# The opening of a Fourier-mixing and SoLU kernel: four z buffers, another order of loads, TensorE transposes for the first units, small operations moved to ScalarE

## The chip, the cores and the metric

The kernel runs on one core of one Trainium2 chip. The metric is the time of one execution on the device in microseconds (us), as the median of several executions.

## The reference

```python
def reference(x, moe_w_in, moe_w_out, moe_g_ln):   # x: 8 x 3136 x 256
    X = np.fft.fft(np.fft.fft(x, axis=1), axis=2).real
    x = X.reshape(8 * 3136, 256)
    h = x @ w_in                                    # 256 x 1024
    e = np.exp(h - h.max(-1, keepdims=True))
    solu = h * (e / (e.sum(-1, keepdims=True) + 1e-09))
    ln = (solu - mean(solu)) / np.sqrt(var(solu) + 1e-06) * g_ln
    return ln @ w_out                               # 1024 x 256
```

The real part of a two-dimensional Fourier transform of each of 8 batches, then a layer of 256 to 1024 to 256 features with a softmax-weighted activation and a normalization.

## The kernel before

The batches are handled in four pairs. The 3136 rows are 49 times 64. For one pair, the rows come in eight chunks. Each chunk is *folded* (mirrored rows and features are added and subtracted, which halves the transform), multiplied by a 49-point table (`transform1`), copied by ScalarE out of PSUM (the memory into which TensorE writes its results) into a buffer `z`, and written to DRAM (`zd`). When all eight chunks are in DRAM, `turn` reads them back in another order (`g`). From there on the work goes by *units*, 25 per pair, 100 in all: second transform (`q`), up-projection (`ps_h`), `ev` (the first VectorE operation of a unit) and `join` on VectorE, `exp` on ScalarE, product on VectorE, square on ScalarE, transpose, and four units later the down-projection. While one pair's units run, the next pair's chunks are folded and transformed in between. Only the first pair has nothing to lie beside, and the weights have to be loaded, narrowed from 64-bit words to float32 and multiplied in that same time: this is the *opening*.

```python
def fold_features(o, i):
    up, down = i[:, :, 1:128], i[:, :, 255:128:-1]
    nc.vector.tensor_tensor(out=o[:, :, 1:128], in0=up, in1=down, op=ALU.add)
    nc.vector.tensor_tensor(out=o[:, :, 129:256], in0=up, in1=down, op=ALU.subtract)
    nc.vector.tensor_copy(out=o[:, :, 0:129:128], in_=i[:, :, 0:129:128])   # the "corner copy"

def transform1(pr, s):
    c, l = divmod(2 * s, CH)                     # chunk, row in it
    if l == 0:
        pr.z = zpool.tile([ZR, CH, D], FP32, tag="z", name="z")      # a pool of 2
    # ... matmuls of F with y = pr.y[c] into ps
    nc.scalar.copy(pr.z[:, l : l + 2, :], ps[0:ZR])
    if l == CH - 2:
        nc.sync.dma_start(out=pr.zd[:, c * CH : (c + 1) * CH, :], in_=pr.z)

# the opening
for c in range(NC):                              # 8 chunks of the first pair
    add_mirror(first, c, nc.vector)
    fold(first, c)
    # ... load of chunk c + 6
    for s in range(CH // 2):
        transform1(first, c * CH // 2 + s)
    if c < 4:
        weights.narrow_in(c)
    # ...
    elif 3 < c < 7:
        weights.product_in(c - 4)
    if c == 5:
        weights.load_out()
weights.place_table()
turn(first, 0)
for i in range(2):
    weights.narrow_out(i)

# the units (cut): i = 0 .. 103
even(cur, up(cur, 0)); odd = up(cur, 1)          # ev on VectorE
take2(nxt, transform2(...)); spread(nxt)
join(cur, odd); expo(cur)
ahead_pe(ahd, cur.k1)                            # transform1 of the next pair
ps_o = [down(old, s) for s in old.signs]         # old = unit i - 4
product(cur, s); square(cur, s); turn_blocks(cur, s)
# ... transposes finished by DMA, statistics
ahead(ahd, cur.k1)                               # loads and folds of the next pair
```

Of the kernel before, what the change touches and what calls it, by code (L numbers as in the profile page):

```python
# [7 lines left out]

# [25 lines left out]
def kernel(  # L34
# [46 lines left out]
    ones = const.tile([P, P], FP32, name="ones")  # L81
    neg_half = const.tile([P, 2], FP32, name="neg_half")
# [33 lines left out]
    def fold_features(o, i):  # L116
        up, down = i[:, :, 1:128], i[:, :, 255:128:-1]
        nc.vector.tensor_tensor(out=o[:, :, 1:128], in0=up, in1=down, op=ALU.add)
        nc.vector.tensor_tensor(out=o[:, :, 129:256], in0=up, in1=down, op=ALU.subtract)  # L119
        nc.vector.tensor_copy(out=o[:, :, 0:129:128], in_=i[:, :, 0:129:128])  # L120
# [19 lines left out]
    def transform1(pr, s):  # L140
# [6 lines left out]
        if l == 0:  # L147
            pr.z = zpool.tile([ZR, CH, D], FP32, tag="z", name="z")
# [69 lines left out]
    def join(t, ps):  # L218
# [9 lines left out]
        nc.vector.tensor_scalar(out=t.neg[:, 0:n], in0=t.nmax[:, 0:n], scalar1=-1.0, scalar2=None, op0=ALU.mult)  # L228
# [39 lines left out]
    class Batch:  # L268


        def __init__(self):
            self.v = fpool.tile([P, 2, FF, 2], FP32, tag="v", name="v32", bufs=2)
            self.uT = fpool.tile([P, 2, KF, 4, 64], FP32, tag="uT", name="uT", bufs=2)
# [6 lines left out]
    def move_blocks(batch, units):  # L280
# [3 lines left out]
        for i in range(4):  # L284
            for q in range(4):
                a, b = slice(32 * i, 32 * i + 32), slice(32 * q, 32 * q + 32)
                nc.sync.dma_start(out=uT[b, i], in_=v[a, q])
# [69 lines left out]
    class Weights:  # L357
# [24 lines left out]
        def load_table(self):  # L382
            self.T = fpool.tile([P, NK, N2], FP32, tag="v", name="T_raw", bufs=2)
            for b in range(2):
                nc.sync.dma_start(out=self.T[b * N2 : (b + 1) * N2], in_=t_tab)

        def place_table(self):
            for b in range(2):
                r = slice(b * N2, (b + 1) * N2)
                nc.scalar.copy(T[r, :, r], self.T[r])  # L390
# [17 lines left out]
        def load_out(self):  # L408
            raw = fpool.tile([P, 2, KF, 4, 64], FP32, tag="uT", name="raw_out", bufs=2)
            self.raw = raw.rearrange("p w c i m -> p (w c i m)").bitcast(I32)  # L410
            for c in range(KF):
                load_piece(moe_w_out, self.raw[:, 2 * c * D : 2 * (c + 1) * D], Wo[:, c], c, 0, D)
# [7 lines left out]
        def centre(self):  # L420
# [5 lines left out]
            for c in range(KF):  # L426
                nc.gpsimd.tensor_tensor(out=Wo[:, c, :], in0=Wo[:, c, :], in1=wbar, op=ALU.subtract)  # L427
# [24 lines left out]
    with tc.manual_schedule():  # L452
        pairs = [Pair(p) for p in range(NP)]
        first, weights = pairs[0], Weights()
        nc.sync.dma_start(out=idx, in_=mirror)

        rooms = {}
        for c in range(2, 6, 2):
            room = fpool.tile([P, 2, KF, 4, 64], FP32, tag="uT", name="room", bufs=2)
            room = room[0:PR].rearrange("p w c i m -> p (w c i m)").rearrange("p (a n) -> p a n", a=4)  # L460
            rooms[c], rooms[c + 1] = [room[:, i] for i in (0, 1)], [room[:, i] for i in (2, 3)]
        load(first, 0)
        nc.sync.dma_start(out=F, in_=f_tab)
        weights.load_in()
        weights.piece_in(0)
        for c in range(1, 4):
            load(first, c, rooms.get(c))
            weights.piece_in(c)
        weights.load_tables()
        for c in range(4, 6):  # L470
            load(first, c, rooms[c])
        nc.vector.memset(ones, 1.0)
# [3 lines left out]
        for c in range(NC):  # L476
            add_mirror(first, c, nc.vector)
            fold(first, c)
            if c + 6 < NC:
                load(first, c + 6)  # L480
            for s in range(CH // 2):
                transform1(first, c * CH // 2 + s)
            if c < 4:
                weights.narrow_in(c)
            if c == 2:
                weights.load_table()
            elif c == 3:
                weights.mid()
            elif 3 < c < 7:
                weights.product_in(c - 4)  # L490
            if c == 5:
                weights.load_out()
        weights.place_table()
        turn(first, 0)
        for i in range(2):
# [6 lines left out]
        lag = 4  # L502
        for i in range(len(units) + lag):
# [4 lines left out]
            last = i >= len(units) - 2  # L508
            if i > lag:
                store(units[i - lag - 1])  # L510
            if cur:
                if i % 2 == 0:
                    batch = Batch()
# [3 lines left out]
            if nxt:  # L517
                take2(nxt, transform2(pairs[nxt.p], nxt.k1))
                spread(nxt)
            if cur:  # L520
# [6 lines left out]
            if cur:  # L527
                for s in cur.signs:
                    product(cur, s)
                for s in cur.signs:  # L530
                    square(cur, s)
                    turn_blocks(cur, s)
            if old:
                scale(old, 0, ps_o[0])
            if cur:
                if last:
                    move_blocks(batch, slice(cur.w, cur.w + 1))
                elif cur.w:
                    move_blocks(batch, slice(0, 2))
                stats(cur)  # L540
            if i < 2:
                weights.narrow_out(i + 2)
            elif i == 2:
# [84 lines left out]
```

## Time and profile before

| | before |
|---|---|
| median | 1234.15 us (3 runs, 1233.82 to 1235.59) |
| span of the profiled run | 1231.2 us |
| last z issued to DRAM | 66.25 us |
| g (first read back) issued | 71.27 us |
| ev of unit 0, VectorE | 81.93 us |
| first transform of the second pair (the "border") | 133.03 us |
| first up-projection of the steady stretch | 139.01 us |
| TensorE's wait in the tail | 2.49 us |

The prediction below shows the views it rests on. One more belongs to the argument: TensorE's timeline in the opening before the change (start, duration, engine, line, operation, tiles, shapes, count, and in brackets the idle time before it and what released it).

```profile
44.58 3.70 PE L158 MATMUL ps<-y,F 98*100 98x258 f32 x8 [3.58 <-DVE y L120]
...
52.93 1.89 PE L158 MATMUL ps<-y,F 98*100 98x258 f32 x8
...
58.10 1.89 PE L158 MATMUL ps<-y,F 98*100 98x258 f32 x8
```

The eight matmuls of one chunk take 3.70 us when TensorE runs at half speed and 1.89 us at full speed; the trace's record of the granted clock has 0.5 from 30.45 us to 50.93 and 1.0 from there to 68.00. So the two late chunks ran at full speed: the weight products stood between them, and TensorE did not pause from 44.58 us on. GpSimd then issues the read back of the transformed rows:

```profile
71.27 2.41 POOL L170 DMA_DIRECT2D g<-zd  x4 [47.83 <-DMA zd<-z]
```

### The profile page before, as it was taken

What the parts mean: (1) busy time and instruction counts of PE and PEld (TensorE: products, weight loads), DVE (VectorE), ACT (ScalarE), POOL (GpSimd) and SP (SyncE); (2) the same over time, 40 slices, a digit from 0 to 9 for tenths busy, and PEclk for the clock granted to TensorE, in tenths of its full rate; (3) what the DMA queues carried; (4) which work ended last, traced back from release to release, by engine and by line L of the source; (5) the groups of instructions that cost most, each with busy time, mean ns of one, the idle gap of its engine ahead of it and who ended that gap; (6) DMA issues with size and microseconds to landing.
All of it is one profiled execution on the core that took longest, in us unless ns stands there. A gap on an engine that the chain in (4) does not pass through costs nothing.

```text
span 1231.2 us, 15674 instructions
## 1 busy us (share of the span) xinstructions
PE 1159.5 (94%) x4664; PEld 875.5 (71%) x4664; DVE 929.2 (75%) x1383; ACT 612.6 (50%) x1151; POOL 542.2 (44%) x964
## 2 busy tenths in 40 slices
PE   2755899999999999999999999999999999999997
PEld 1423577777777777777777777777777777777786
DVE  6658887777777887787677887777777788778770
ACT  1223555555554555555454565565554555555551
POOL 2014755444453554544364554544453333333331
PEclk9677899999999999999999999999999999999999
DMA  9737899797899798886899899987899677776765
GB/s 230 205 118 132 156 177 162 163 169 138 147 185 181 144 172 175 165 171 115 151 189 193 141 174 173 162 168 134 150 176 163 113 125 128 122 135 106 133 111 106
DMA packets 476372, 189.57 MB, mean 154 GB/s; under 512 B 444566, under 2 KB 458142, under 8 KB 476288
## 3 DMA queue, kind: packets, MB, share of 16 engines
q1 hardware_dynamic: 462464, 150.02, 70.1%
q0 software_dynamic: 13824, 38.55, 12.0%
q8 instruction: 38, 0.62, 0.2%
q14 instruction: 46, 0.38, 0.1%
HBM read 44.78 MB, written 38.80 MB: 68 GB/s over the span
## 4 chain that ended last, share of the span: by engine, by line
PE 88%; DVE 6%; DMA 2%; issue 2%; POOL 1%; ACT 1%; POOLq 0%; DVEq 0%; ACTq 0%
PE ps_o L293 53%; PE ps_h L209 26%; PE ps L158 4%; PE ps L181 3%; DVE h L223 1%; PE wps L405 1%; DVE u L242 1%; DMA xb<-in_x_dram,idx 1%; ACT u L234 1%; DVE tmp L331 1%; DVE v L278 1%; POOL Wo L427 1%; DVE y L119 0%; DVE tmp L344 0%; DMA zd<-z 0%
## 5 line engine op out<-in xcount | busy, mean ns | idle before, releaser
L293 PE MATMUL ps_o<-Wo,uT 128*128 128x256 f32 x3136 | 694.0, 379 | 2.5 <-DMA uT<-v 2.5
L293 PEld LDWEIGHTS ps_o<-Wo,uT 128*128 128x128 f32 x3136 | 612.4, 197 | 64.7 <-issue 3.6
L209 PE MATMUL ps_h<-Wi,q 128*128 128x512 f32 x800 | 367.0, 602 | 12.7 <-DVE ev L215 12.7
L242 DVE SCALAR_TENSOR_TENSOR u<-h,u 128x1024 f32<-128x1024 f32 x196 | 233.6, 1228 | 139.3 <-ACT u L234 139.3
L234 ACT ACTIVATE u<-h,neg 128x1024 f32<-128x1024 f32 x196 | 223.7, 1142 | 223.6 <-DVE neg L228 223.6
L251 ACT ACTIVATE h<-u,nmean 128x1024 f32<-128x1024 f32 x196 | 223.6, 1142 | 130.2 <-POOL nmean L244 130.2
L244 POOL TENSOR_SCALAR nmean<-usum 128x1 f32<-128x1 f32 x196 | 126.9, 648 | 363.6 <-DVE u L242 363.3
L209 PEld LDWEIGHTS ps_h<-Wi,q 128*128 128x128 f32 x800 | 154.4, 194 | 165.7 <-issue 156.3
L223 DVE CUSTOM_DVE_ANT_0 h<-ev,ps_h 128x1024 f32<-128x1024 f32 x196 | 231.7, 1219 | 44.6 <-PE ps_h L209 39.2
L278 DVE STREAM_TRANSPOSE v<-u 128x1024 f32<-128x1024 f32 x200 | 238.1, 1234 | 0.1
L215 DVE SCALAR_TENSOR_TENSOR ev<-w_mid,r,ps_h 128x1024 f32<-128x1024 f32 x100 | 127.6, 1276 | 58.4 <-PE ps_h L209 55.3
L187 ACT COPY q<-ps 128x256 f32<-128x256 f32 x100 | 37.1, 371 | 180.4 <-PE ps L181 173.5
L305 POOL DMA_INDIRECT out_dram<-ot,idx x96 | 102.7, 1069 | 44.0 <-issue 24.0
L158 PE MATMUL ps<-y,F 98*100 98x258 f32 (+3 forms) x288 | 76.4, 402 | 36.5 <-DVE y L120 36.1
L263 POOL TENSOR_SCALAR v<-ssq 128x2 f32<-128x2 f32 (+1 forms) x100 | 27.8, 278 | 169.4 <-ACT h L251 169.4
L181 PEld LDWEIGHTS ps<-T,g 128*128 128x128 f32 x400 | 60.9, 194 | 58.1 <-issue 55.9
L298 ACT ACTIVATE ot<-ps_o,rs 128x256 f32<-128x256 f32 x196 | 80.9, 457 | 27.2 <-PE ps_o L293 27.2
L158 PEld LDWEIGHTS ps<-y,F 98*100 98x100 f32 x288 | 47.2, 183 | 51.4 <-DVE y L120 26.6
L266 POOL TENSOR_TENSOR rs<-v,neg_half 128x2 f32<-128x2 f32 (+1 forms) x100 | 72.9, 729 | 7.8
L170 POOL DMA_DIRECT2D g<-zd x80 | 47.8, 604 | 56.0 <-DMA zd<-z 47.8
L181 PE MATMUL ps<-T,g 128*128 128x128 f32 x400 | 61.6, 278 | 10.8 <-DMA g<-zd 10.8
L161 ACT COPY z<-ps 100x512 f32<-100x512 f32 x64 | 36.3, 570 | 42.4 <-PE ps L158 25.2
(58 smaller groups left out, 421.7 us busy)
## 6 DMA issues: line engine op xcount, KB each, us to landing
uT<-v SPq DMA_DIRECT2D x784, 128.0 KB
zd<-z SPq DMA_DIRECT2D x32, 400.0 KB
g<-zd POOLq DMA_DIRECT2D x80, 160.0 KB, 5.4
out_dram<-ot SPq DMA_DIRECT2D x100, 128.0 KB
xa<-in_x_dram SPq DMA_DIRECT2D x28, 392.0 KB
raw_in<-in_moe_w_in_dram SPq DMA_DIRECT2D x4, 512.0 KB
raw_out<-in_moe_w_out_dram SPq DMA_DIRECT2D x8, 256.0 KB
uT<-v SPq DMA_DIRECT2D x32, 64.0 KB
```

The source lines that it names most:

```text
L158: nc.tensor.matmul(o[..., cs], F[:, 2 * t + h, :], i[..., cs], start=first, stop=True, skip_group_check=True)
L181: nc.tensor.matmul(ps[:, h * P : (h + 1) * P], g[:, k, h * P : (h + 1) * P], T[:, k1, :], start=(h == 0), stop=True, skip_group_check=True)
L209: nc.tensor.matmul(ps[:, fs], t.q[:, c * P : (c + 1) * P], Wi[:, c, fs], start=True, stop=True)
L215: nc.vector.scalar_tensor_tensor(out=t.ev, in0=w_mid, scalar=t.r, in1=ps, op0=ALU.mult, op1=ALU.add)
L223: nc.vector.tensor_tensor_reduce(out=t.h[s], in0=t.ev, in1=ps, scale=1.0, scalar=-3.0e38, op0=ALU.subtract if s else ALU.add, op1=ALU.max, ...
L234: nc.scalar.activation(out=t.u[s], in_=t.h[s], func=ACT.Exp, bias=t.neg[:, s : s + 1], accum_out=t.esum[:, s : s + 1])
L242: nc.vector.scalar_tensor_tensor(out=t.u[s], in0=t.h[s], scalar=1.0, in1=t.u[s], op0=ALU.mult, op1=ALU.mult, accum_out=t.usum[:, s : s + 1])
L244: nc.gpsimd.tensor_scalar(out=t.nmean[:, s : s + 1], in0=t.usum[:, s : s + 1], scalar1=-1.0 / FF, scalar2=None, op0=ALU.mult)
L251: nc.scalar.activation(out=t.h[s], in_=t.u[s], func=ACT.Square, bias=t.nmean[:, s : s + 1], accum_out=t.ssq[:, s : s + 1])
L278: nc.vector.transpose(out=t.batch.v[:, t.w, :, o], in_=t.u[s])
L293: nc.tensor.matmul(ps, uT[:, c, :, s], Wo[:, c, :], start=(c == 0), stop=(c == KF - 1))
L305: dma = nc.gpsimd.indirect_dma_start(out=out, out_offset=bass.IndirectOffsetOnAxis(ap=idx[:, i : i + 1], axis=0), in_=t.ot[s], in_offset=None)
```

## The change

Its intent is a shorter opening: do not let ScalarE wait for one of two z buffers, load what is needed first, take half of w_out out of the way of the last z writes, let TensorE transpose the first four units (VectorE sets their pace), and relieve VectorE of small operations. The diff, cut to its core:

```diff
 def fold_features(o, i):
-    nc.vector.tensor_copy(out=o[:, :, 0:129:128], in_=i[:, :, 0:129:128])
+    nc.scalar.copy(o[:, :, 0:129:128], i[:, :, 0:129:128])
 # transform1
-    pr.z = zpool.tile([ZR, CH, D], FP32, tag="z", name="z")
+    if pr.p == 0 and c % 2:
+        z = fpool.tile([P, FF], FP32, tag="u", name="z_u", bufs=2)
+        pr.z = z[0:ZR].rearrange("p (l d) -> p l d", l=CH)
+    else:
+        pr.z = zpool.tile([ZR, CH, D], FP32, tag="z", name="z")
 # join
-    nc.vector.tensor_scalar(out=t.neg[:, 0:n], in0=t.nmax[:, 0:n], scalar1=-1.0, ...)
+    nc.scalar.mul(out=t.neg[:, 0:n], in_=t.nmax[:, 0:n], mul=-1.0)
+def turn_whole(t):              # units 0 to 3: 8 blocks of 128x128 for each sign
+    for s in t.signs:
+        for half in range(2):
+            ps = ps_m.tile([P, n, P], FP32, tag="m", name="ps_t")
+            for c in range(n):
+                nc.tensor.matmul(ps[:, c, :], t.u[s][:, ...], ident, is_transpose=True, ...)
+            nc.scalar.copy(uT[:, half * n : (half + 1) * n, :, s], ps)
 # load_table: one copy of the table instead of two
 # load_out: w_out in two transfers of four row blocks, load_out(0) and load_out(1)
 # centre
-    for c in range(KF):
-        nc.gpsimd.tensor_tensor(out=Wo[:, c, :], in0=Wo[:, c, :], in1=wbar, op=ALU.subtract)
+    nc.vector.tensor_tensor(out=Wo, in0=Wo, in1=wbar (broadcast), op=ALU.subtract)
 # the opening (the loads are also reordered: w_in pieces ahead of x chunks, tables last)
 for c in range(NC):
+    if c < 4:
+        weights.narrow_in(c)
     add_mirror(first, c, nc.vector)
     fold(first, c)
+    if c == 1:
+        weights.load_table()
+    elif c == 3:
+        weights.place_out(); weights.load_out(0); weights.mid(); weights.scale_out()
     for s in range(CH // 2):
         transform1(first, c * CH // 2 + s)
-    if c < 4: weights.narrow_in(c)
-    elif 3 < c < 7: weights.product_in(c - 4)
-    if c == 5: weights.load_out()
+weights.load_out(1)
+turn(first, 0)
 weights.place_table()
-turn(first, 0)
-for i in range(2): weights.narrow_out(i)
+for h in range(3): weights.product_in(h)
+for i in range(4): weights.narrow_out(i)
 # units 0 to 3: turn_whole for the unit before, ahead of join; no turn_blocks, no move_blocks
 # the last unit's moves alternate between SyncE and GpSimd
```

(Cuts and condensations marked by comments; helper definitions left out.)

More of the change, by code (lines that the diff above doesn't have):

```diff
@@ L7 @@
 from concourse._compat import with_exitstack
+from concourse.masks import make_identity
 FP32 = mybir.dt.float32
@@ L81 @@
     ones = const.tile([P, P], FP32, name="ones")
+    ident = const.tile([P, P], FP32, name="ident")
     neg_half = const.tile([P, 2], FP32, name="neg_half")
@@ L227, in join @@
         t.neg = small.tile([P, 2], FP32, tag="neg", name="neg")
-        nc.vector.tensor_scalar(out=t.neg[:, 0:n], in0=t.nmax[:, 0:n], scalar1=-1.0, scalar2=None, op0=ALU.mult)
+        nc.scalar.mul(out=t.neg[:, 0:n], in_=t.nmax[:, 0:n], mul=-1.0)
     def expo(t):
@@ L268, with __init__ @@
     class Batch:
-        def __init__(self):
-            self.v = fpool.tile([P, 2, FF, 2], FP32, tag="v", name="v32", bufs=2)
+        def __init__(self, by_blocks):
+            if by_blocks:
+                self.v = fpool.tile([P, 2, FF, 2], FP32, tag="v", name="v32", bufs=2)
             self.uT = fpool.tile([P, 2, KF, 4, 64], FP32, tag="uT", name="uT", bufs=2)
@@ L278, in turn_blocks, with move_blocks @@
             nc.vector.transpose(out=t.batch.v[:, t.w, :, o], in_=t.u[s])
-    def move_blocks(batch, units):
+    def turn_whole(t):
+        uT = t.batch.uT[:, t.w].rearrange("p c i (n s) -> p c (i n) s", s=2)
+        n = KF // 2
+        for s in t.signs:
+            for half in range(2):
+                ps = ps_m.tile([P, n, P], FP32, tag="m", name="ps_t")
+                for c in range(n):
+                    f = half * n + c
+                    nc.tensor.matmul(ps[:, c, :], t.u[s][:, f * P : (f + 1) * P], ident, is_transpose=True,
+                                     start=(c == 0), stop=(c == n - 1), skip_group_check=True)
+                nc.scalar.copy(uT[:, half * n : (half + 1) * n, :, s], ps)
+    def move_blocks(batch, units, engines=(nc.sync,)):
         v = batch.v[:, units].rearrange("p w (c q n) s -> p q (w c) (n s)", q=4, n=32)
@@ L286, in move_blocks @@
                 a, b = slice(32 * i, 32 * i + 32), slice(32 * q, 32 * q + 32)
-                nc.sync.dma_start(out=uT[b, i], in_=v[a, q])
+                engines[i % len(engines)].dma_start(out=uT[b, i], in_=v[a, q])
     def down(t, s):
@@ L383, in load_table @@
             self.T = fpool.tile([P, NK, N2], FP32, tag="v", name="T_raw", bufs=2)
-            for b in range(2):
-                nc.sync.dma_start(out=self.T[b * N2 : (b + 1) * N2], in_=t_tab)
+            nc.sync.dma_start(out=self.T[0:N2], in_=t_tab)
         def place_table(self):
@@ L389, in place_table @@
                 r = slice(b * N2, (b + 1) * N2)
-                nc.scalar.copy(T[r, :, r], self.T[r])
+                nc.scalar.copy(T[r, :, r], self.T[0:N2])
         def mid(self):
@@ L406, in product_in, with place_out, load_out, scale_out @@
             nc.scalar.copy(w_mid if h == KD else Wi[:, h, :], ps)
-        def load_out(self):
+        def place_out(self):
             raw = fpool.tile([P, 2, KF, 4, 64], FP32, tag="uT", name="raw_out", bufs=2)
             self.raw = raw.rearrange("p w c i m -> p (w c i m)").bitcast(I32)
-            for c in range(KF):
-                load_piece(moe_w_out, self.raw[:, 2 * c * D : 2 * (c + 1) * D], Wo[:, c], c, 0, D)
+        def load_out(self, part):
+            c = slice(part * KF // 2, (part + 1) * KF // 2)
+            if moe_w_out.dtype == FP32:
+                nc.sync.dma_start(out=Wo[:, c], in_=moe_w_out.rearrange("(c p) f -> p c f", p=P)[:, c])
+            else:
+                nc.sync.dma_start(out=self.raw.rearrange("p (c f) -> p c f", c=KF)[:, c],
+                                  in_=moe_w_out.bitcast(I32).rearrange("(c p) f -> p c f", p=P)[:, c])
+        def scale_out(self):
             nc.vector.tensor_scalar(out=g_ln, in0=g_ln, scalar1=2.0 ** -20, scalar2=None, op0=ALU.mult)
@@ L425, in centre @@
             nc.scalar.mul(out=wbar, in_=cs, mul=1.0 / FF)
-            for c in range(KF):
-                nc.gpsimd.tensor_tensor(out=Wo[:, c, :], in0=Wo[:, c, :], in1=wbar, op=ALU.subtract)
+            nc.vector.tensor_tensor(out=Wo, in0=Wo, in1=wbar.unsqueeze(1).to_broadcast([P, KF, D]), op=ALU.subtract)
     def ahead(pr, step):
@@ L455 @@
         nc.sync.dma_start(out=idx, in_=mirror)
+        make_identity(nc, ident)
         rooms = {}
@@ L461 @@
             rooms[c], rooms[c + 1] = [room[:, i] for i in (0, 1)], [room[:, i] for i in (2, 3)]
+        weights.load_in()
+        weights.piece_in(0)
         load(first, 0)
         nc.sync.dma_start(out=F, in_=f_tab)
-        weights.load_in()
-        weights.piece_in(0)
         for c in range(1, 4):
+            weights.piece_in(c)
             load(first, c, rooms.get(c))
-            weights.piece_in(c)
-        weights.load_tables()
         for c in range(4, 6):
             load(first, c, rooms[c])
+        weights.load_tables()
         nc.vector.memset(ones, 1.0)
@@ L480 @@
                 load(first, c + 6)
+            if c == 1:
+                weights.load_table()
+            elif c == 3:
+                weights.place_out()
+                weights.load_out(0)
+                weights.mid()
+                weights.scale_out()
             for s in range(CH // 2):
                 transform1(first, c * CH // 2 + s)
-            if c < 4:
-                weights.narrow_in(c)
-            if c == 2:
-                weights.load_table()
-            elif c == 3:
-                weights.mid()
-            elif 3 < c < 7:
-                weights.product_in(c - 4)
-            if c == 5:
-                weights.load_out()
+        weights.load_out(1)
+        turn(first, 0)
         weights.place_table()
-        turn(first, 0)
-        for i in range(2):
+        for h in range(3):
+            weights.product_in(h)
+        for i in range(KF * D // NW):
             weights.narrow_out(i)
@@ L502 @@
         lag = 4
+        whole = 4
         for i in range(len(units) + lag):
@@ L508 @@
             last = i >= len(units) - 2
+            prv = units[i - 1] if 0 < i <= whole else None
             if i > lag:
@@ L512 @@
                 if i % 2 == 0:
-                    batch = Batch()
+                    batch = Batch(i >= whole)
                 cur.batch, cur.w = batch, i % 2
@@ L519 @@
                 spread(nxt)
+            if prv:
+                turn_whole(prv)
             if cur:
@@ L531 @@
                     square(cur, s)
-                    turn_blocks(cur, s)
+                    if i >= whole:
+                        turn_blocks(cur, s)
             if old:
@@ L536 @@
                 if last:
-                    move_blocks(batch, slice(cur.w, cur.w + 1))
-                elif cur.w:
+                    move_blocks(batch, slice(cur.w, cur.w + 1), (nc.sync, nc.gpsimd) if cur.w else (nc.sync,))
+                elif cur.w and i >= whole:
                     move_blocks(batch, slice(0, 2))
                 stats(cur)
-            if i < 2:
-                weights.narrow_out(i + 2)
-            elif i == 2:
+            if i == 0:
                 weights.centre()
```

## The prediction

> **What bounds the kernel now.** I read the page's slices first, then TensorE's timeline, then the chain of waits over the first 144 us, then the stretches, then the tail.
>
> ```profile
> PE   2755899999999999999999999999999999999997
> PEclk9677899999999999999999999999999999999999
> ```
>
> A slice is 30.8 us. From the fifth on TensorE is full; before that it is a quarter to half busy, partly at half clock. TensorE's own timeline gives the border:
>
> ```profile
> 120.09 6.62 PE L209 MATMUL ps_h<-Wi,q 128*128 128x512 f32 x8 [4.73 <-DVE ev L215]
> 126.55 0.61 PE L181 MATMUL ps<-T,g 128*128 128x128 f32 x4
> 133.03 2.03 PE L158 MATMUL ps<-y,F 98*100 98x258 f32 x4 [5.87 <-DVE y L120]
> 134.85 4.32 PE L293 MATMUL ps_o<-Wo,uT 128*128 128x256 f32 x16
> 139.01 3.60 PE L209 MATMUL ps_h<-Wi,q 128*128 128x512 f32 x8
> ...
> 1219.40 7.15 PE L293 MATMUL ps_o<-Wo,uT 128*128 128x256 f32 x32 [2.49 <-DMA uT<-v]
> ```
>
> Columns: start, time, engine, line, operation, in brackets the idle time before and its releaser. From 133 us to the end TensorE never waits again except 2.49 us in the tail: one unit follows another every 11.65 us. So a gain in VectorE, ScalarE or DMA time after 133 us is worth nothing, and the change is worth what it moves this border forward, plus the tail. The chain shows what sets the border:
>
> ```profile
> 66.25 4.31 DMA zd<-z
> 73.10 3.18 DMA g<-zd
> 78.47 5.09 PE ps_h L209 x8
> 120.39 6.47 POOL Wo L427 x8
> ```
>
> The last z must be written to DRAM (landed at 66.25 + 4.31 = 70.56), read back turned (g, 76.3), and multiplied before VectorE starts unit 0 at 81.93. Then four units run with no down-projection to fill TensorE, at VectorE's pace: its ev starts lie at 81.93, 94.39, 108.73, 118.71 and 132.87 us, 51 us for four units. The 6.47 us of GpSimd delay the last of them.
>
> Why is z so late? ScalarE's timeline and the stretches:
>
> ```profile
> 41.38 1.07 ACT L161 COPY z<-ps 100x512 f32<-100x512 f32 x2 [13.65 <-DMA zd<-z]
> ```
>
> ```profile
> core 0: us, PE busy (x) PEld busy (x) DVE busy (x) ACT busy (x) POOL busy (x), PEclk, DMA share, GB/s
> 0.00:10.00 10.00, 0.00 (x0) 0.00 (x0) 3.05 (x4) 1.28 (x1) 5.78 (x10) 1.00 0.79 205
> 10.00:20.00 10.00, 3.40 (x8) 2.15 (x8) 6.04 (x12) 0.59 (x1) 1.52 (x2) 1.00 1.04 274
> 20.00:30.00 10.00, 3.96 (x9) 2.04 (x8) 9.73 (x19) 1.76 (x3) 1.18 (x1) 0.83 1.01 215
> 30.00:40.00 10.00, 6.37 (x15) 4.01 (x16) 9.61 (x21) 0.00 (x0) 0.00 (x0) 0.52 0.91 233
> 40.00:50.00 10.00, 6.42 (x14) 3.61 (x13) 9.87 (x21) 3.32 (x6) 0.00 (x0) 0.50 0.75 216
> 50.00:60.00 10.00, 10.00 (x31) 5.56 (x31) 2.47 (x8) 3.59 (x5) 0.00 (x0) 0.95 0.47 148
> 60.00:70.00 10.00, 5.61 (x24) 3.25 (x23) 8.08 (x17) 5.62 (x6) 0.00 (x0) 0.90 0.73 249
> ```
>
> ScalarE waits 13.65 us for the first of two z buffers, because z queues behind loads. DMA is saturated to 40 us (share about 1, mean of four rows 232 GB/s) and slack from 40 to 70 (0.65): there the kernel waits for z buffers, and TensorE makes the three weight products (3.43 to 5 us each) between the last transforms.
>
> [...] the trace has 0.59 for a z copy (about 0.54 when they follow each other), and I use 0.54.
>
> **The change part by part.**
>
> Folding. VectorE narrows a piece of w_in in 4.35 us (16.33 to 20.68) and folds a chunk in 2.5. The first fold still waits for the gathered xb at about 13.8 us, but the first narrowing now goes ahead of it: 4.35 us earlier. The tables land late now (about 38 us, the end of the saturated stretch), so the fifth chunk starts near 38.4 instead of 41.74, and the last ends near 49. With four z buffers and the products moved behind the transforms, no wait of TensorE stands between (4.23 us before the last chunk today).
>
> Last z. DMA moved 205+274+215+233+216+148+249, times 10 us, 15.4 MB, up to 70 us. The second copy of the table (0.41 MB) goes and half of w_out (1.05 MB) moves behind the last z: 13.9 MB are left, at 232 GB/s 60 us. Computed work would allow about 59 (the last z needs the buffer of chunk 3, whose write queues behind the first half of w_out until about 53; two copies, then 4.3 us). So the last z lands at about 60.5 instead of 70.56, DMA-bound.
>
> Unit 0. From z to ev(0) it takes 81.93 - 70.56 = 11.4 us today: about 72[...]. The other way in: the second half of w_out lands at about 64, and VectorE then needs two narrowings of 4.55 (61.47 to 70.6 for two): 73. I take ev(0) at 73, a gain of 9.
>
> Units 0 to 3. Unit 0: 5.7 us to its product, then the centring: cs on TensorE (16 instructions, some 3.5), ready early; ScalarE's square and wbar to 80.7, one VectorE subtraction of 2048 elements, 2.2 us (1020 elements take 1.21): ev(1) at 83, 10 us instead of 12.46. Unit 1 without transposes (2.37) has VectorE work of 9.98 - 2.3 = 7.65: ev(2) at 90.6. Units 2 and 3 are ScalarE's: two exps 2.3, wait for the mean 1.4, two squares 2.3, q 0.37, four PSUM copies of 2.2, neg 0.25, in order: about 9.0 each, and 1.3 for the fold in unit 3. ev(4) at about 110, 37 us after ev(0) instead of 51.
>
> The border. Unit 3's transposes now stand ahead of the first transform and down-projection on TensorE: 16 blocks, 3.5 us if one costs two instructions of 0.11 as the 128x128 matmuls of L181 do, and the last group waits for a PSUM buffer until ScalarE has done unit 3's squares, near 112. So the transform starts near 114 instead of 133.03, 19 earlier, and ramps up the clock once less deep, 1 to 2 us. Gain of the opening: 20.
>
> Tail. The last unit's sixteen moves take SyncE 10.4 us; half on GpSimd saves 5, but TensorE waits only 2.49 there, since unit 98's matmuls end at 1216.9: gain 2.5.
>
> VectorE's small operations (0.17 for neg, 0.08 to 0.2 for the corner copies) lie beside TensorE's 11.65 per unit after the border: 0.
>
> Sum: 1234.15 - 20 - 2.5 = 1211.7, call it 1212.
>
> **The rivals.** (a) The transposes cost more than I allow: a cold clock doubles them (the stretch from 40 to 50 us ran at 0.50), and ScalarE's copies write every second element. Then units 2 to 4 are 1 to 2 us longer each, 1216 or so. For it: TensorE is idle a third of that time.[...] (b) The last z doesn't land earlier: [...]w_out's second half delays g and the narrowing; the first half of w_out stands ahead of four z writes. Then 1217 to 1219. Against: the slack from 40 to 60 us. (c) ScalarE becomes the bound later, or the corner copies reach TensorE late: a few tenths in each of 24 folds, 2 to 5 us. Against: ScalarE is half busy in steady state (5 to 6 of each 10 us) and TensorE's transforms have their y a fold ahead. (d) Better than thought: DMA keeps 274 GB/s, as from 10 to 20 us; z lands at 55 to 57 and the narrowing ends sooner; 1206 to 1208.
>
> **Range and chances.** The DMA estimate is good to 3 us, the four units to 3, the border to 2: together about 5. So 1212, with 1204 to 1221 holding it 8 times in 10. Two per cent is 1209.5, half a deviation below: faster 0.33, same 0.66, slower 0.01, as nothing after the border gets more TensorE work.
>
> **What would show it.** Right: TensorE's last wait before the steady stretch ends at 112 to 115; g<-zd is issued near 61; ev(0) near 73, then spacings of 10, 7.7, 9, 10; no ScalarE wait of over 5 us for zd; the tail's 2.49 gone; the stretch between the border and the tail as long as before. Wrong: TensorE waits appearing after 115 us, a unit spacing of 11 or more among the first four, or g issued after 66.

What is cut from it is 0.5 us on the way from z to unit 0 (72.5 with it), which the other way in, 73, covers. The "1 to 2 us" for the clock at the border is the author's estimate, and the trace of the kernel before has what it is about: after the wait of 5.87 us the granted clock was 0.50 (129.5 to 136.2 us), the first four transforms took 2.03 us and the sixteen down-projections 4.32.

## The result, and the profile after

| | before | after | predicted |
|---|---|---|---|
| median | 1234.87 us (4 runs) | 1214.41 us (4 runs, 1211.9 to 1215.37) | 1212 (1204 to 1221) |
| ratio to before, 95% interval | | 0.9828 (0.9807 to 0.985) | |
| span of the profiled run | 1231.2 | 1212.1 | |
| last z issued | 66.25 | 60.02 | about 56 (landed 60.5) |
| g issued | 71.27 | 65.16 | near 61 |
| ev of unit 0 | 81.93 | 78.91 | 73 |
| ev of unit 4 | 132.87 | 116.72 | 110 |
| border | 133.03 | 119.04 | 114 |
| first up-projection after it | 139.01 | 123.44 | |

A ratio is the mean time of one kernel's fast runs over that of the other's fast runs of the same rounds, so it is not quite the ratio of the medians quoted beside it. The result is within 2% of before: 1.7% faster, with an interval that ends just short of 2%.

In the 40 slices of the page TensorE is now seven or eight tenths busy from the second slice and full from the fifth. The row of granted clock shows no half-speed slice, but it cannot be used for the opening (see below):

```profile
PE   2787999999999999999999999999999999999998
PEclk9998999999999999999999999999999999999999
```

The border, in TensorE's timeline after the change (L297 are the transposes, L165 the transform that was L158, L216 the up-projection that was L209):

```profile
118.50 0.66 PE L297 MATMUL ps_t<-ident,u 128*128 128x128 f32 x4 [2.19 <-ACT q L194]
119.04 1.11 PE L165 MATMUL ps<-y,F 98*100 98x258 f32 x4
...
123.44 3.60 PE L216 MATMUL ps_h<-Wi,q 128*128 128x512 f32 x8
```

From here to the end the same work follows as from 139.01 us before. TensorE's last wait before the steady stretch is the 2.19 us ahead of the transposes. The up-projection starts 139.01 - 123.44 = 15.57 us earlier. The tail has no wait left; the last down-projections run in one piece:

```profile
1172.35 34.87 PE L314 MATMUL ps_o<-Wo,uT 128*128 128x256 f32 x160
```

So 15.57 us come from the opening and 2.49 from the tail, 18.06 of the 19.1 us between the two spans. Most of the other 1.04 us lies in the steady stretch: between 140 and 1180 us TensorE was busy 1039.22 us before and 1040.00 after. The missing 0.78 us are two waits of the kernel before, ahead of the third transform of the third pair and of the fourth pair:

```profile
435.67 1.08 PE L158 MATMUL ps<-y,F 98*100 98x258 f32 x4 [0.40 <-ACT q L187]
...
716.83 1.08 PE L158 MATMUL ps<-y,F 98*100 98x258 f32 x4 [0.38 <-DVE y L120]
```

The changed kernel has neither; 0.26 us stay unassigned. VectorE's busy time over the whole run fell from 929.2 to 903.2 us and ScalarE's rose from 612.6 to 644.8. So moving small operations off VectorE was predicted to be worth nothing after the border, and it was worth next to nothing. (With the corner copies back on VectorE, in run e1 below, the two waits are back with 0.23 and 0.19 us.)

The opening gained four microseconds less than predicted. (The chain of waits of this run is empty, with shares of 0%, so it cannot be used; the queues have to be read.) TensorE's timeline shows where they are missing:

```profile
41.27 3.70 PE L165 MATMUL ps<-y,F 98*100 98x258 f32 x8 [1.01 <-DVE y L120]
45.76 3.73 PE L165 MATMUL ps<-y,F 98*100 98x258 f32 x8 [0.78 <-ACT y L122]
50.27 3.73 PE L165 MATMUL ps<-y,F 98*100 98x258 f32 x8 [0.78 <-ACT y L122]
54.78 4.59 PE L165 MATMUL ps<-y,F 98*100 98x258 f32 x16 [0.79 <-ACT y L122]
```

The last four chunks start 4.5 us apart. Each runs at half speed (3.7 us for eight matmuls, 1.89 at full speed; the last has four such and twelve smaller ones, 4.59 us in all; before the change the same sixteen took 2.35 us, at full speed). The last three each wait 0.78 us for the corner copy (L122), which is now a ScalarE operation. The wait looks harmless, but ScalarE's timeline shows what it is part of:

```profile
47.84 0.59 ACT L168 COPY z_u<-ps 100x512 f32<-100x512 f32 x1 [2.14 <-PE ps L165]
49.52 0.59 ACT L168 COPY z_u<-ps 100x512 f32<-100x512 f32 x1 [1.10 <-PE ps L165]
50.01 0.21 ACT L122 COPY y<-xa 98x8 f32<-98x8 f32 x1
```

The z copies (L168) of a chunk wait for TensorE. The corner copy of the *next* chunk stands behind them in ScalarE's queue and runs in order, at 50.01 us; TensorE starts that next chunk at 50.27. The corner copies of the last four chunks (40.78, 45.49, 50.01 and 54.52 us) each start about 0.1 us before the end of the z copy ahead of them. So TensorE waits for ScalarE and ScalarE for TensorE: a ring. VectorE had gone ahead; it began to narrow w_out at 51.94 us, before TensorE began the last chunk.

The second consequence is on the w_out side. SyncE issues, in order, the last z and then the second half of w_out; GpSimd issues g when the z has landed:

```profile
60.02 0.28 SPq L170 DMA_DIRECT2D zd<-z_u  x1
60.35 0.39 SPq L437 DMA_DIRECT2D raw_out<-in_moe_w_out_dram  x1
```

```profile
65.16 2.42 POOL L177 DMA_DIRECT2D g<-zd  x4 [41.74 <-DMA zd<-z_u]
```

and VectorE waits for that half before it can narrow it and start unit 0:

```profile
69.81 0.43 DVE L352 TENSOR_SCALAR tmp<-raw_out 128x512 int32<-128x512 int32 x1 [8.68 <-DMA raw_out<-in_moe_w_out_dram]
...
78.91 1.27 DVE L222 SCALAR_TENSOR_TENSOR ev<-w_mid,r,ps_h 128x1024 f32<-128x1024 f32 x1
```

Two narrowings fill the 9.1 us between these two lines without a gap. DMA was not the limit before that; in the stretch just ahead of the last z it was at less than half:

```profile
core 0: us, PE busy (x) PEld busy (x) DVE busy (x) ACT busy (x) POOL busy (x), PEclk, DMA share, GB/s
...
50.00:60.00 10.00, 8.95 (x26) 6.43 (x27) 8.91 (x20) 2.76 (x9) 0.00 (x0) 1.00 0.47 180
```

Note the 1.00 under PEclk, beside matmuls that take twice as long as at full speed. The trace's own record of the clock begins only at 59.77 us, with the change to full speed, and the view shows 1.00 where there is no record yet; before that the durations have to be read. They agree with the record: the matmuls are at half speed up to the end of the last chunk. (The expectations of e1 and e8 below put this change at 56.6 us. There the twelve smaller matmuls begin, which take less time each; their starts lie 0.21 us apart here, and 0.11 in the kernel before, where they ran at full speed.)

Why pauses of 0.78 us go together with a clock at half speed is not shown. In the traces of the two kernels the record changes at whole multiples of 3.41 us. In the changed kernel the first change to full speed, at 59.77 us, ends a step in which TensorE had no pause (56.36 to 59.77 us, inside the burst that begins at 54.78); the fullest step before it, 46.12 to 49.53 us, was busy 3.37 of 3.41 us. In the kernel before, the steps from 16.80 and from 47.52 us had no pause and full speed followed, but the one from 30.45 us had none either and half speed followed. So no rule can be read from it. That the ring's pauses hold TensorE at half speed is the author's theory at this point; e1 and e10 below take the pauses out.

A smaller difference is in units 0 to 3. The ev starts lie at 78.91, 88.48, 96.11, 104.68 and 116.72 us. The first three spacings, 9.57, 7.63 and 8.57 us, are the predicted 10, 7.7 and 9.0 or better; the fourth is 12.04 instead of 10. In unit 3 VectorE's first product takes 3.51 us where its others take 1.23:

```profile
110.93 3.51 DVE L249 SCALAR_TENSOR_TENSOR u<-h,u 128x1024 f32<-128x1024 f32 x1 [2.41 <-ACT u L241]
```

and GpSimd's timeline at that moment has the first `add_mirror` of the second pair:

```profile
110.98 2.37 POOL L129 TENSOR_TENSOR xa<-xa,xb 98x1020 f32<-98x1020 f32 x1
113.30 1.21 POOL L130 TENSOR_TENSOR xa<-xa,xb 98x4 f32<-98x4 f32 x1
```

The two run side by side, and the product is longer by 3.51 - 1.23 = 2.28 us, about the 2.37 us of the addition; in e2 below, with this addition moved to VectorE, it takes 1.23 us again. The one-column addition after it (L130) takes 1.21 us here; its median on GpSimd over the run is 0.20.

### The profile page after: what moved, and what is told of

The parts are those of the page before. It is cut to its first block, busy times and chain, and to the rows that moved or that the text cites. A ratio compares the mean times of both kernels' runs of the same rounds, so it can differ in the third digit from the quotient of the medians.

```text
span 1212.1 us, 15808 instructions
## 1 busy us (share of the span) xinstructions
PE 1166.4 (96%) x4720; PEld 881.5 (73%) x4720; DVE 903.2 (75%) x1240; ACT 644.8 (53%) x1301; POOL 544.0 (45%) x966
## 5 line engine op out<-in xcount | busy, mean ns | idle before, releaser
L216 PE MATMUL ps_h<-Wi,q 128*128 128x512 f32 x800 | 364.5, 599 | 2.4 <-DVE ev L222 2.4
L216 PEld LDWEIGHTS ps_h<-Wi,q 128*128 128x128 f32 x800 | 153.4, 192 | 153.7 <-issue 146.2
L286 DVE STREAM_TRANSPOSE v<-u 128x1024 f32<-128x1024 f32 x192 | 227.9, 1227 | 0.1
L235 ACT ACTIVATE neg<-nmax 128x2 f32<-128x2 f32 (+1 forms) x100 | 20.4, 204 | 176.1 <-DVE nmax L230 176.1
L165 PE MATMUL ps<-y,F 98*100 98x258 f32 (+3 forms) x288 | 81.4, 423 | 28.8 <-DVE y L120 26.5
L165 PEld LDWEIGHTS ps<-y,F 98*100 98x100 f32 x288 | 50.2, 196 | 45.3 <-ACT y L122 34.0
L273 POOL TENSOR_TENSOR rs<-v,neg_half 128x2 f32<-128x2 f32 (+1 forms) x100 | 72.5, 725 | 7.8
```

Source lines behind the costliest of these rows:

```text
L165: nc.tensor.matmul(o[..., cs], F[:, 2 * t + h, :], i[..., cs], start=first, stop=True, skip_group_check=True)
L216: nc.tensor.matmul(ps[:, fs], t.q[:, c * P : (c + 1) * P], Wi[:, c, fs], start=True, stop=True)
L286: nc.vector.transpose(out=t.batch.v[:, t.w, :, o], in_=t.u[s])
```

## The experiments

The theory after reading the traces was: (A) the ring of corner copies on ScalarE keeps TensorE at half speed through the last chunks, so the last z, and all behind it, is late. Its rival: DMA sets the last z, as the prediction said, or the second half of w_out does. Further questions: (C) what the four z buffers are worth, (E) whether GpSimd's addition in unit 3 costs time, later (G) whether the worth of the z buffers depends on the ring. Where an expectation uses a letter, it means these.

All kernels gave correct results. The edits are relative to the changed kernel, the ratios to the kernel before on the same chip. Differences told below are those of the medians; the kernels ran on several chips, and differences of ratios or of profiled spans can be 1 or 2 us smaller or larger.

| run | edit | median us | ratio | 95% interval |
|---|---|---|---|---|
| after | | 1214.41 | 0.9828 | 0.9807 to 0.985 |
| e1 | corner copy on VectorE | 1209.43 | 0.9803 | 0.9784 to 0.9821 |
| e2 | unit 3's addition on VectorE | 1213.04 | 0.9836 | 0.9817 to 0.9856 |
| e3 | two z buffers | 1223.66 | 0.9916 | 0.99 to 0.9933 |
| e4 | no TensorE transposes | 1216.88 | 0.9862 | 0.9846 to 0.9879 |
| e5 | second half of w_out early | 1210.66 | 0.9809 | 0.9793 to 0.9826 |
| e6 | e1 and e2 | 1207.28 | 0.979 | 0.9773 to 0.9807 |
| e7 | e1, e2 and e5 | 1208.64 | 0.9799 | 0.9781 to 0.9817 |
| e8 | products between the transforms | 1222.37 | 0.9913 | 0.9896 to 0.993 |
| e9 | e1 and e3 | 1216.26 | 0.9859 | 0.9844 to 0.9875 |
| e10 | transforms issued one fold late | 1206.28 | 0.9773 | 0.9753 to 0.9792 |
| e11 | e10 and e2 | 1204.93 | 0.976 | 0.9746 to 0.9773 |

**e1: the corner copy back on VectorE.**

```diff
-        nc.scalar.copy(o[:, :, 0:129:128], i[:, :, 0:129:128])
+        nc.vector.tensor_copy(out=o[:, :, 0:129:128], in_=i[:, :, 0:129:128])
```

> The changed kernel, but the two corner columns of every fold are copied by VectorE again. Theory A (the ring): in the changed kernel the corner copy stands in ScalarE's queue behind the z copies of the chunk before, so TensorE waits 0.78 us ahead of each of the last chunks[...] and stays at half speed (3.70 us a chunk, 4.5 us from chunk to chunk) until 56.6 us. Then with this edit the last chunks follow each other without the 0.78 us waits, TensorE reaches full speed before 52 us, the last z is issued near 55.5 instead of 60.0, lands near 60 instead of 64.5, ev(0) comes at 73 to 75 instead of 78.9, and the whole is 4 to 5 us faster than the changed kernel (ratio to before about 0.979). Theory B (DMA sets z, as the prediction had it): z lands at 63 to 64.5 whatever TensorE does, ev(0) stays within 1.5 us of 78.9, ratio stays at 0.982 to 0.984.

Measured: 1209.43 us, 5.0 less than the changed kernel. TensorE's timeline in the opening:

```profile
42.46 7.23 PE L165 MATMUL ps<-y,F 98*100 98x258 f32 x24 [1.15 <-DVE y L122]
50.05 2.39 PE L165 MATMUL ps<-y,F 98*100 98x258 f32 x16 [0.37 <-DVE y L122]
```

The waits of 0.78 us are gone. Three chunks run in 7.23 us without a pause, where they took 3.70 + 3.73 + 3.73 us and two waits; the last z is issued at 55.30 us instead of 60.02, and VectorE's next line follows from it:

```profile
73.01 1.28 DVE L222 SCALAR_TENSOR_TENSOR ev<-w_mid,r,ps_h 128x1024 f32<-128x1024 f32 x1
```

The border comes at 113.03 us instead of 119.04. Theory A holds. (The two intervals of the ratio overlap a little, 0.9807 to 0.9821, so it is the trace that decides here.) With the ring gone, ScalarE again waits for z buffers, 1.68, 0.46 and 3.12 us: now DMA is what holds it.

**e5: the second half of w_out right behind the first.** If DMA had room and only the order of issue made w_out late, this must help too.

```diff
             elif c == 3:
                 weights.load_out(0)
+                weights.load_out(1)
 ...
-        weights.load_out(1)
```

> The changed kernel, but the second half of w_out is loaded right behind the first, ahead of the writes of the last five z chunks. Theory A (TensorE paces z, DMA has room from 50 to 60 us): the last z is issued at 60 and lands at 64.5 as before, the narrowing of w_out ends near 70.5 instead of 78.8, and ev(0) is set by g and the first up-projection, at 76 to 77.5 instead of 78.9: 1.5 to 2.5 us faster than the changed kernel. Theory B (DMA sets z): the megabyte ahead of the z writes pushes the last z to 67 or later, ev(0) to 79 or later, no gain or up to 3 us slower.

Measured: 1210.66 us, 3.8 less, where I had expected 1.5 to 2.5. The last z is issued at 59.38 us, no later than in the changed kernel although 1.05 MB more went ahead of it, so DMA did have room. The ring is still there, with the same waits of 0.78 us. Unit 0 starts at 73.57 us; VectorE now waits 3.64 us for the up-projection instead of 8.68 us for w_out. So ev(0) has two ways in, and in the changed kernel w_out is the later one. Part of the gain was not foreseen: g comes so soon after the weight products that TensorE has no wait there (2.32 us in the changed kernel), and the first up-projection takes 3.70 us instead of 5.39.

**e10: the ring taken apart by order alone.** Is it ScalarE as an engine, or the place in its queue? Here the corner copies stay on ScalarE, but the transforms of a chunk are issued after the fold of the next one, so its corner copy stands *ahead* of the z copies that wait for TensorE.

```diff
             if c + 6 < NC:
                 load(first, c + 6)
+            for s in range(CH // 2 if c else 0):
+                transform1(first, (c - 1) * CH // 2 + s)
 ...
-            for s in range(CH // 2):
-                transform1(first, c * CH // 2 + s)
+        for s in range(CH // 2):
+            transform1(first, (NC - 1) * CH // 2 + s)
```

> The changed kernel with the corner copies still on ScalarE, but in the opening each chunk's transforms are written into the program one chunk later, after the next chunk's fold; so in ScalarE's queue the corner copy of a chunk now stands ahead of the z copies of the chunk before. If it is the place in the queue that makes the ring (theory A), TensorE's 0.78 us waits for the corner copy are gone, it reaches full speed before 53 us, the last z is issued at 55 to 57, ev(0) comes near 73 to 74.5, and the run gains 4 to 5 us on the changed kernel like the run with the corners on VectorE. If it is ScalarE itself (a slower or later copy), TensorE keeps waiting for it and the last z stays at 59 or later.

Measured: 1206.28 us, 8.1 less than the changed kernel (6.4 between the spans), and faster than before by over 2%. TensorE's timeline:

```profile
36.09 10.46 PE L165 MATMUL ps<-y,F 98*100 98x258 f32 x32 [3.15 <-ACT z L168]
46.80 2.49 PE L165 MATMUL ps<-y,F 98*100 98x258 f32 x16 [0.24 <-ACT y L122]
```

The last z is issued at 52.38 us, earlier than the expected 55 to 57; ev(0) starts at 70.16, the border comes at 110.67. Of TensorE's waits for the corner copy one of 0.24 us is left. The same 0.2 us copies on the same engine cost next to nothing when they do not stand behind work that waits for their own consumer. It was the place in the queue.

Not all of the 8.1 us is the ring. VectorE began to fold the fifth chunk at 37.23 us here and at 39.09 in the changed kernel, mostly because a table (Q) came sooner: VectorE waited 0.22 us for it instead of 1.61. That is not the edit; in e11, with the same opening, the fold began at 39.38. Counted from this fold, the last z is issued 20.93 us later in the changed kernel, 15.68 in e1, 15.15 in e10 and 14.34 in e11: without the ring 5.3 to 6.6 us sooner.

**e3: two z buffers.**

```diff
-            if pr.p == 0 and c % 2:
+            if False:
```

> The changed kernel with two z buffers instead of four. Theory A (TensorE at half speed and the corner copies pace the last chunks anyway): ScalarE waits for z writes again (up to 10 us for the first), but the last z is issued only 1 to 3 us later than 60.0, and the whole loses 1 to 3 us. Theory C (the z waits were what held the opening): the last z is issued at 65 or later, and the whole loses 5 us or more against the changed kernel.

Measured: 1223.66 us, 9.2 more; I had expected 1 to 3. The last z is issued at 67.47 us. ScalarE's timeline has the wait of the kernel before again:

```profile
41.09 1.07 ACT L168 COPY z<-ps 100x512 f32<-100x512 f32 x2 [12.05 <-DMA zd<-z]
```

TensorE waits 8.96 us ahead of the chunk at 42.32 us, the next chunk starts 6.4 us after that one, and the three behind it go through the ring at 4.5 us each, so the time lost is never made up: ev(0) starts at 87.05 us. That suggested that the cost depends on the ring.

**e9: two z buffers, corner copies on VectorE.** The edits of e1 and e3 together.

> Two z buffers and the corner columns on VectorE. With the corner copies on ScalarE, going from four z buffers to two cost 9 us (I had expected 1 to 3). Theory G: part of those 9 us are the ring again (ScalarE's wait for a z buffer holds up the next corner copy and so TensorE). Then here TensorE works ahead into its four PSUM buffers while ScalarE waits; the z buffers alone set the last z, issued at 59 to 61.5 instead of 55.3 with four buffers, and the whole is 4 to 6 us slower than the run with the corners on VectorE and four buffers, about level with the changed kernel (1214 to 1216 us). Theory C (z buffers alone cost the 9 us): the last z at 63 or later, 1218 us or more.

Measured: 1216.26 us, 6.8 more than e1, against 9.2 more with the ring (span against span: 1212.8 - 1207.2 = 5.6, against 1221.8 - 1212.1 = 9.7). ScalarE's first wait is as long, 13.35 us, but without the ring TensorE catches up part of it: the last three chunks, with 32 matmuls, in 8.14 us from 47.79 (in the changed kernel from 45.76 to 59.37), and the last z is issued at 58.81. So the four buffers are worth 5.6 to 6.8 us by themselves and more than 9 beside the ring.

**e4: no transposes on TensorE.** Units 0 to 3 go through VectorE and DMA as all the others do.

```diff
-        whole = 4
+        whole = 0
```

> The changed kernel, but all units are transposed in blocks by VectorE and DMA (the first four no longer by TensorE). Theory A (VectorE's pace sets units 0 to 3): ev spacings go from 9.6, 7.6, 8.6, 12.0 to about 12, 10, 10, 11.5, ev(4) comes near 122.5 instead of 116.7; TensorE's first transform of the second pair no longer waits behind transposes (2.3 us from ev(4) now, about 0.2 then), so the border moves from 119.0 to about 122.7: 3 to 4 us slower than the changed kernel. Theory D (the gain came from elsewhere: narrowing and centring taken out of the units): within 1.5 us of the changed kernel.

Measured: 1216.88 us, 2.5 more (the spans say the same: 1214.6 against 1212.1); I had expected 3 to 4. The first three spacings of ev are 9.96, 9.91 and 9.92 us, against 9.57, 7.63 and 8.57: the transposes on TensorE save 4.0 us there, and ev(4) came 3.67 us later without them. But the first up-projection after the border is only 126.14 - 123.44 = 2.70 us later, because in the changed kernel unit 3's transposes themselves stand ahead of the border. The transposes are a small part of the gain.

**e2: the addition in unit 3 on VectorE.**

```diff
-                add_mirror(pr, c, nc.gpsimd)
+                add_mirror(pr, c, nc.vector if pr.p == 1 and c == 0 else nc.gpsimd)
```

> The changed kernel, but the first add_mirror of the second pair runs on VectorE instead of GpSimd. Theory E[...]: in the changed kernel unit 3's first product on VectorE takes 3.51 us instead of 1.23 because GpSimd's add of 1020 elements runs beside it, and GpSimd's mean for that unit comes late behind the same add, so the fourth unit spacing is 12.0 us instead of 10. Then here the product takes 1.23 us again, the add fits into VectorE's wait for ScalarE's exp (2.4 us), the fourth spacing falls to 9.5 to 10.5, and the border (first transform of the second pair) moves forward 2 to 3 us: 2 to 3 us faster than the changed kernel. Theory F (the product is slow for another reason, such as the DMA writes of the new x chunks): the product stays above 2 us and the spacing at 12.

Measured: 1213.04 us, which the intervals do not separate from the changed kernel. VectorE's timeline shows the effect all the same:

```profile
112.17 1.23 DVE L249 SCALAR_TENSOR_TENSOR u<-h,u 128x1024 f32<-128x1024 f32 x1 [1.54 <-ACT u L241]
```

The product takes 1.23 us again, the fourth spacing 8.85 instead of 12.04, while the third grows to 9.79 because the addition is in it. From ev(0) to the border it is 117.99 - 79.82 = 38.2 us instead of 40.1. Here ev(0) itself was 0.9 us later, so 1 us was left. The cause is shown; its worth of 1 to 2 us is at the edge of what three rounds resolve.

**e6: e1 and e2 together, e7: e1, e2 and e5 together.** Do the gains add?

> Both: corner columns on VectorE, and the second pair's first add_mirror on VectorE. If the two effects are independent they add up: ev(0) near 73, fourth spacing near 10, border near 110.5 instead of 119.0, the whole 7 us faster than the changed kernel, near 1207 us or 0.978 of before. If the border is then held by something else (the last transposes' PSUM buffer behind ScalarE's squares), only 5 us.

> Corner columns and first add on VectorE, and the second half of w_out loaded behind the first. With TensorE no longer the pace, DMA now is: the extra megabyte ahead of the z writes delays the write of chunk 3, on whose buffer the last z waits (3.1 us already in the run with the corners alone), so the last z is issued at 57.5 to 58.5 instead of 55.3, g comes 2 to 3 us later, and ev(0) is set by g near 74 to 76 instead of 73: equal to or up to 2 us slower than the run without this edit, where on the unchanged corner copies the same edit gained 3.8 us. If TensorE still set the pace, it would gain again 2 us or more.

Measured: e6 1207.28 us, 7.1 less than the changed kernel and about the sum of the two; e7 1208.64 us. In e6 the border is at 111.52 us, 1.5 earlier than in e1. In e7 the early half of w_out adds nothing: ScalarE waits 7.09 us for a z buffer, the last z is issued at 58.98 us and ev(0) starts at 73.26 against 73.47 in e6 (74 to 76 were expected). Without the ring DMA has no more room, and the two ways into ev(0) are level. The intervals of e6 and e7 overlap, so neither order of w_out is shown to be better once the ring is gone.

**e8: the weight products between the transforms, as before.**

```diff
+            if 3 < c < 7:
+                weights.product_in(c - 4)
 ...
-        for h in range(3):
-            weights.product_in(h)
```

> The changed kernel with the three weight products back between the last transforms, as before the change. They fill TensorE and bring it to full speed earlier (near 50 us instead of 56.6), but put 3.4 to 4.8 us of product and 1 us of ScalarE copy ahead of each later chunk: the last z is issued at 64 to 68 instead of 60.0, ev(0) at 82 to 86 instead of 78.9, and the whole is 3 to 6 us slower than the changed kernel. If the clock is all that matters, it loses nothing.

Measured: 1222.37 us, 8.0 more; I had expected 3 to 6. TensorE's timeline:

```profile
57.97 1.97 PE L165 MATMUL ps<-y,F 98*100 98x258 f32 x8 [1.21 <-ACT y L122]
59.78 3.60 PE L425 MATMUL wps<-w_in,w_mid 128*128 128x512 f32 x8
```

With the products between them the chunks run at full speed (1.97 us each), but the products also go into the ring: a period is now 6.6 us (57.97 from 51.35) instead of 4.5, and the last z is issued at 67.66. The bursts are now 5.4 us long, and of the three products the first takes 4.62 us (from 45.53) and the other two 3.60. The half speed alone is therefore not the whole cost of the ring: a chunk at full speed still has its 1.21 us of wait and everything that TensorE does in between.

**e11: the version put together, e10 and e2.**

> The version put together from what held: transforms issued one fold late (the last run with that edit: 1206.28, ratio 0.9773) and the first fold of unit 3 on VectorE. If the two gains lie one after the other, as the units 0 to 3 follow the opening: ev(0) near 70, the fourth spacing near 9 instead of 12, the border near 108 to 109, 1 to 2 us less: 1204 to 1205.5, ratio 0.976. If the second gain is within the noise again, as it was for the fold alone, 1206 to 1207 and the trace alone shows it (unit 3's first product 1.23 us instead of over 3).

Measured: 1204.93 us, ratio 0.976, its whole interval beyond 2%: this version beats both kernels. The border comes at 110.04 us and the next up-projection at 114.44, 4.40 later. In e10 that took 116.71 - 110.67 = 6.04 us, slower at first: the four transforms took 1.91 us there and 1.11 here, the sixteen down-projections 4.49 and 3.62. That makes 1.64 us. The opening itself ended later than in e10 (ev(0) at 71.92 instead of 70.16, for the reason told under e10), so the spans differ by only 2.6 us (1205.7 and 1203.1), while the way from ev(0) to this up-projection took 46.55 us in e10 and 42.52 here.

## Why the prediction was right or wrong

As a whole it was right: 1212 us predicted, 1214.41 measured, within the range, and within 2% of before, to which it gave the largest chance. By its steps:

- *What bounds the kernel, and that only the border and the tail count.* Right but for 0.78 us: 18.06 of 19.1 us are found at the border and in the tail. "TensorE never waits again except 2.49 us" overlooks the two waits at 435.67 and 716.83 us. Two readings beside it are off, without consequence: in the slices shown TensorE is at seven tenths in the second and full from the sixth, and the 11.65 us from unit to unit hold only where the next pair's transforms stand between; elsewhere it is mostly 10.79.
- *"With four z buffers and the products moved behind the transforms, no wait of TensorE stands between."* Wrong, and this is the step that failed. Three waits of 0.78 us stand there, with TensorE at half speed around them. (The 4.23 us named there are VectorE's wait for TensorE; of that wait 1.82 us are left.) The prediction priced the corner copies at "0" because they lie beside TensorE's work after the border, and its rival (c) looked for late corner copies in the 24 later folds. They cost nothing there; they cost in the last chunks of the opening, where the one queue ties them to TensorE.
- *"So the last z lands at about 60.5 instead of 70.56, DMA-bound."* The size of this term is wrong by some 4 us: issued at 60.02 us, it landed shortly before g was issued at 65.16. And it was not bound by DMA (share 0.47 in the ten microseconds before), but by the ring. In e1, without the ring, the last z is issued at 55.30 us, ev(0) starts at 73.01 and the border is at 113.03; the prediction had 73 and 114. Rival (b), "the last z doesn't land earlier", came half true: z was late because of the ring and not because of DMA, but the narrowing of w_out's second half did hold up unit 0, as (b) allowed.
- *"The other way in: the second half of w_out lands at about 64": 73.* The mechanism was right: two narrowings behind that landing set ev(0), to 0.1 us. The landing was near 69.8. About 4 us of this miss are carried on from the step before, since the transfer is issued behind the last z; the rest is that the transfer took 9.4 us. It is the reason for 78.91 instead of 73.
- *Units 0 to 3: 10, 7.7, 9.0, about 10.* 9.57, 7.63, 8.57, 12.04. The first three are right. The fourth was sized with 1.3 us for the fold, and the longer first product beside GpSimd's addition (3.51 us instead of 1.23) was left out; e2 shows it.
- *Transposes: two instructions of 0.11 us for a block, 3.5 us for a unit.* Half of it was right: a block takes one instruction (56 records for the 56 blocks of units 0 to 3), eight in a row took 1.04 us (from 86.41), 0.13 each, and unit 3's 16 take 1.80 + 0.66 = 2.46 us. The wait of the last group for a PSUM buffer was predicted and is there, 2.19 us. From ev(4) to the border it was 119.04 - 116.72 = 2.3 us instead of 4.
- *Clock at the border, 1 to 2 us.* Right: from the border to the next up-projection 4.40 us instead of 139.01 - 133.03 = 5.98, which is 1.58; the four transforms took 1.11 us instead of 2.03, the sixteen down-projections 3.62 instead of 4.32.
- *Tail 2.5 us.* Right: 2.49, though no run undid this edit alone.
- *The signs of being wrong.* One came true, "a unit spacing of 11 or more among the first four": the fourth, 12.04 us.

The sum was 20 + 2.5; it came to 15.57 + 2.49, and 0.78 and 0.26 besides. The miss of the first term is the z that the ring held; ev(0) came 5.9 us later than predicted, and the first up-projection after the border 4.4; the shorter transposes and the clock made good the rest. That the total is nearer than the terms is luck: the 0.78 us had not been predicted, and the medians differ by 20.46 us where the profiled runs differ by 19.1.

What stays open: why the clock stayed at half speed. The runs show only what went together: full speed in e1 and e10, where the pauses are gone, and in e8, with longer but rarer pauses (1.21 us in 6.6); no run was made to test the clock alone. The worth of the new order of loads, of the single copy of the table, of the centring on VectorE and of the tail's moves was not measured one by one, and 0.26 us of the gain have no place.

## What to carry to other kernels

Giving a small operation to an engine with time to spare also gives it a place in that engine's queue. Here it stood behind operations that wait for the consumer of its own result, the two engines ran in a ring, and the cost was not its 0.2 us but the pace of everything in the ring: 4.5 us a chunk, and 5.0 us of 1214 by e1. Move the operation ahead of those waits (here by issuing the transforms one fold late) before changing engines. And in an opening, list every way into the first unit with its last arrival; a gain on one way is worth only what the next one leaves.
